# k loaded for two groups at a time in rows of two tokens, turned and pooled by head halves

## The chip, the cores and the metric

The kernel runs on one core of one Trainium2 chip. The metric is device time in microseconds, the median of several executions. Engines are named as the profile names them: PE multiplies matrices (PEld loads its weights), DVE, ACT and POOL work on tiles, and SP only issues DMAs.

## The reference, cut to what matters

Attention over keys and values that are averaged over eight tokens, then two feed-forward layers (the first one without an activation between its products):

```python
batch, n_heads, seq, head_dim = (8, 8, 576, 64)
k_p = k.reshape(B, H, Sp, pool, D).mean(axis=3)          # pool = 8, Sp = 72
v_p = v.reshape(B, H, Sp, pool, D).mean(axis=3)
scores = scale * np.matmul(q, k_p.transpose(0, 1, 3, 2))
scores = scores - np.max(scores, axis=-1, keepdims=True)
attn = np.exp(scores)
attn = attn / (np.sum(attn, axis=-1, keepdims=True) + 1e-09)
out = np.matmul(attn, v_p)                               # to 4608 tokens x 512
x = (x @ w1) * (x @ w2) @ w3 @ w_out                     # 512 -> 1024 -> 512
h = x @ w_in
x = (h * (1.0 / (1.0 + np.exp(-1.702 * h)))) @ w_out2    # 512 -> 2048 -> 512
```

All data are float32. q and k are drawn eight times wider than the other inputs.

## The kernel before, in words

**Groups.** Attention is worked in 32 groups; a group n is two heads of one batch element (`divmod(n, HP)` with four pairs of heads). The steps of a group are functions: `g_load` (k and q), `g0` (turn and pool k, turn q), `g1` (scores and their maximum), `g2` (exponential), `g3` (sum and division), `g_va` and `g_vb` (pooled values), `g4` (probabilities turned and split in two parts), `g6` (probabilities times values, written into the slots of x). `tick_first` and `tick` call them one after another, one tick at a time, between the steps of the weights.

**k in a group.** `load_blocks` (L229) issues four DMAs for k and four for q, each for 32 partitions: partition t holds token 32 g + t, for one head and one half of its 64 elements. So each piece of memory that is read is 32 floats, 128 bytes. DVE turns the 32 x 32 blocks (L255 for k, L256 for q), so that the head's elements lie on the partitions and the tokens along the row, and sums each eight tokens (L258). ACT copies the sums of head 0 and head 1 into a block matrix `kbd` (L260, L261), with zeros elsewhere, so that one product with the turned q gives the scores of both heads (L277).

```python
kbd = pa.tile([P, 2, SK], F32, name="kbd")
nc.scalar.copy(kbd[:D, 0], ks[:D])
nc.scalar.copy(kbd[D:, 1], ks[D:])
g_load(n + 1)
```

The raw k and q share one tag of four buffers, which is two groups of each. v is loaded by L249 and L250 into a single buffer, at the end of `g_va` of the group before.

**Weights.** At the same time `Conv` loads the weights (L151; 40 loads of 512 KB in this first stage, 24 with rows of 4 KB and 16 with pieces of 1 KB) and converts each on ACT (L166, L168), DVE (L169) and POOL (L172), then splits it in a high and a low part (L104 on ACT, L105 on DVE or POOL). Each product of two float32 matrices is three products of these parts (L114, L115, L116). The weight stage first multiplies w3 by w_out: w3 is turned on PE (L508), and for each of eight row blocks 24 products sum into one bank `acc`. Then the blocks of 512 tokens pass through w1, w2 and the product of the weights (the loop over `blk` and `f`, L602), with two ticks of attention in each step. The last stage, from about 600 us on, prepares and computes the second layer (`bk` in the rows).

**Order.** The instructions of each engine and the issues of each DMA queue are put in order when the kernel is built, by a scheduler that simulates the program's instructions with their dependences (`schedule_with_timeline_sim=True`). On the chip each engine runs its own list in that order and waits by semaphores. So a changed duration or dependence at one place can move instructions elsewhere. Nearly all DMAs are issued by SP.

Of the kernel before, what the change touches and what calls it, by code (L numbers as in the profile page):

```python
# [7 lines left out]
F32 = mybir.dt.float32  # L8
# [4 lines left out]
ALU = mybir.AluOpType  # L13
AX = mybir.AxisListType
# [3 lines left out]
P = 128  # L18
# [4 lines left out]
def pooled_attention_moe_moe2(  # L23
# [167 lines left out]
    with pa_ctx:  # L191
# [13 lines left out]
        nc.vector.memset(qT[:, S:], 0.0)  # L205
        kbd = pa.tile([P, 2, SK], F32, name="kbd")
        nc.vector.memset(kbd, 0.0)
        s_sl = take(dtype=F32)
# [15 lines left out]

        g_q, g_k, g_v, g_s = {}, {}, {}, {}

        def load_blocks(dst, src, b, hp):
            for c in range(4):
                nc.sync.dma_start(  # L229
                    dst[32 * c:32 * c + 32],  # L230
                    src[b, 2 * hp + c // 2, :, 32 * (c % 2):32 * (c % 2) + 32].rearrange(
                        "(g t) d -> t g d", t=32))

        def g_load(n):
            if n >= NG:
                return
            b, hp = divmod(n, HP)
            g_k[n] = pa.tile([P, S], F32, name="kr", tag="raw", bufs=4).rearrange("p (g d) -> p g d", d=32)
            load_blocks(g_k[n], k, b, hp)
            g_q[n] = pa.tile([P, S], F32, name="qr", tag="raw", bufs=4).rearrange("p (g d) -> p g d", d=32)  # L240
            load_blocks(g_q[n], q, b, hp)
# [10 lines left out]
        def g0(n):  # L252
            kr, qr = g_k.pop(n), g_q.pop(n)
            kT = pa.tile([P, S], F32, name="kT", tag="kT")
            nc.vector.transpose(out=kT, in_=kr.rearrange("p g d -> p (g d)"))  # L255
            nc.vector.transpose(out=qT[:, :S], in_=qr.rearrange("p g d -> p (g d)"))  # L256
            ks = pa.tile([P, SK], F32, name="ks", tag="ks")
            nc.vector.tensor_reduce(  # L258
                out=ks, in_=kT.rearrange("p (s u) -> p s u", u=POOL), op=ALU.add, axis=AX.X)
            nc.scalar.copy(kbd[:D, 0], ks[:D])  # L260
            nc.scalar.copy(kbd[D:, 1], ks[D:])  # L261
            g_load(n + 1)
# [7 lines left out]
        def g1(n):  # L270
            sc, s_t = banks_of(n), s_of(n)
            mov = kbd.rearrange("p a s -> p (a s)")
            nm = pa.tile([P, 2 * TT], F32, name="nm", tag="nm", bufs=2)
# [288 lines left out]

        conv.load()
        g_load(0)
        v_load(0)
# [563 lines left out]
```

## Time and profile before

| what | value |
|---|---|
| median of three runs | 1477.42 us (1476.0 to 1481.82) |
| the profiled execution | 1479.71 us, of which the span of the profile 1478.0 us |
| PE busy | 1438.7 us (97% of the span) |
| DVE, ACT, POOL busy | 988.7, 693.9 and 489.0 us |
| mean granted clock of PE | 0.993 of full speed |
| packets of the DMA engines | 294,436, of them 201,664 under 512 bytes |
| read and written in HBM | 209.72 and 56.62 MB |

The page of the profile gives the busy time of each engine, its busy tenths in 40 equal slices of the span, and the chain of work that ended last. "Releaser" is what ended an idle time. The DMA share is the mean busy share of the core's 16 DMA engines; it can be over 1 in a short stretch, since packets overlap.

### The profile page before, as it was taken

To read this page: it belongs to the slowest core of one execution; us is meant where nothing else is said; L and a number is where in the kernel's file an instruction comes from. 1 tells how busy PE (TensorE), PEld (TensorE's weight loads), DVE (VectorE), ACT (ScalarE), POOL (GpSimd) and SP (SyncE) were. 2 spreads that over 40 slices of the span, in tenths; PEclk is the share of its full clock that TensorE was granted. 3 is DMA by queue.
4 is the path that set the end of the run, shared out by engine and by line. 5 is a ranking of instruction groups with operands and counts; after the bars stand their busy time and mean duration, and the time that the engine had idled before them with its cause. 6 is when DMAs were issued, how large, how long until landed. Compare 5 with 4: busy or idle time off the path is not lost.

```text
span 1478.0 us, 19436 instructions
## 1 busy us (share of the span) xinstructions
PE 1438.7 (97%) x6536; PEld 1190.0 (81%) x6536; DVE 988.7 (67%) x1728; ACT 693.9 (47%) x1212; POOL 489.0 (33%) x589
## 2 busy tenths in 40 slices
PE   6979999999999999999999999999999999999998
PEld 4867888888888888888788887888788888888886
DVE  7888998878787877654737255683559354944554
ACT  7875444434343433366635344552455244534442
POOL 8789656554545555366733100000000000000000
PEclk9989999999999999999999999999999999999999
DMA  9992233323232311199879978877677766785665
GB/s 265 248 233 48 57 85 57 80 46 78 49 77 49 77 33 37 42 325 344 309 236 398 325 243 276 294 211 221 194 244 224 221 197 221 239 234 180 194 213 139
DMA packets 294436, 267.64 MB, mean 181 GB/s; under 512 B 201664, under 2 KB 226240, under 8 KB 294336
## 3 DMA queue, kind: packets, MB, share of 16 engines
q1 hardware_dynamic: 291648, 265.09, 59.8%
q10 hardware_dynamic: 2688, 1.31, 0.3%
q8 instruction: 52, 0.85, 0.2%
q14 instruction: 48, 0.39, 0.1%
HBM read 209.72 MB, written 56.62 MB: 180 GB/s over the span
## 4 chain that ended last, share of the span: by engine, by line
PE 82%; DMA 7%; DVE 5%; ACT 2%; SPq 2%; issue 1%; POOL 1%; DVEq 0%; ACTq 0%; POOLq 0%
PE bk L709 39%; PE wk L114 8%; PE wk L115 8%; PE wk L116 8%; PE acc L114 4%; PE acc L115 4%; PE acc L116 4%; PE wk L277 2%; DMA wud<-wt 2%; DVE p L314 1%; SPq L229 1%; DMA st<-wind 1%; PE bk L115 1%; PE bk L116 1%; PE bk L114 1%
## 5 line engine op out<-in xcount | busy, mean ns | idle before, releaser
L709 PE MATMUL bk<-mv,st 128*128 128x512 f32 x1152 | 272.6, 391 | 0.7 <-DMA st<-wud 0.7
L709 PE MATMUL bk<-xM,st 128*128 128x512 f32 x1092 | 259.0, 390 | 3.9 <-DMA st<-wind 3.7
L709 PEld LDWEIGHTS bk<-mv,st 128*128 128x128 f32 x1152 | 217.3, 189 | 46.3 <-issue 1.1
L709 PEld LDWEIGHTS bk<-xM,st 128*128 128x128 f32 x1092 | 204.5, 188 | 48.6 <-issue 2.5
L114 PE MATMUL wk<-s,s 128*128 128x512 f32 x576 | 227.0, 396 | 2.8 <-DVE a L641 1.2
L116 PE MATMUL wk<-s,s 128*128 128x512 f32 x576 | 224.9, 391 | 2.1 <-DVE s L105 2.1
L115 PE MATMUL wk<-s,s 128*128 128x512 f32 x576 | 224.9, 391 | 0.0
L314 DVE STREAM_TRANSPOSE p<-s_t 32x160 f32<-32x160 f32 (+1 forms) x560 | 178.5, 319 | 10.3
L114 PE MATMUL acc<-s,s 128*128 128x512 f32 x352 | 134.8, 406 | 8.2 <-ACT s L104 3.2
L115 PE MATMUL acc<-s,s 128*128 128x512 f32 x352 | 141.4, 402 | 0.9 <-POOL s L105 0.8
L116 PE MATMUL acc<-s,s 128*128 128x512 f32 x352 | 140.4, 399 | 0.0
L114 PEld LDWEIGHTS wk<-s,s 128*128 128x128 f32 x576 | 108.5, 189 | 26.2 <-DVE a L641 2.1
L116 PEld LDWEIGHTS wk<-s,s 128*128 128x128 f32 x576 | 108.3, 188 | 24.8 <-DVE s L105 2.3
L115 PEld LDWEIGHTS wk<-s,s 128*128 128x128 f32 x576 | 108.4, 188 | 22.1 <-DVE s L391 0.4
L105 DVE TENSOR_TENSOR mv<-g,mv 128x1024 fp32r<-128x1024 f32 x80 | 97.8, 1222 | 33.6 <-ACT mv L104 32.2
L104 ACT CAST mv<-g 128x1024 fp32r<-128x1024 f32 x80 | 84.3, 1054 | 71.8 <-PE bk L709 71.4
L172 POOL TENSOR_TENSOR cv<-cv,s 128x512 int32<-128x512 int32 x72 | 97.5, 1364 | 28.6 <-DVE cv L169 21.1
L105 POOL TENSOR_TENSOR s<-a,s 128x512 fp32r<-128x512 f32 x56 | 72.5, 1294 | 82.5 <-ACT s L104 62.7
L638 ACT COPY a<-wk 128x512 f32<-128x512 f32 x72 | 42.1, 585 | 110.5 <-PE wk L116 89.7
L369 POOL TENSOR_TENSOR ph<-p,ph 128x576 fp32r<-128x576 f32 x32 | 45.7, 1429 | 126.5 <-ACT ph L368 123.9
L114 PEld LDWEIGHTS acc<-s,s 128*128 128x128 f32 x352 | 67.8, 193 | 23.4 <-ACT s L104 5.2
L115 PEld LDWEIGHTS acc<-s,s 128*128 128x128 f32 x352 | 68.2, 194 | 15.0 <-POOL s L105 2.0
(190 smaller groups left out, 2357.9 us busy)
## 6 DMA issues: line engine op xcount, KB each, us to landing
st<-wud SPq DMA_DIRECT2D x96, 512.0 KB, 4.4
st<-wind SPq DMA_DIRECT2D x66, 512.0 KB, 4.7
st<-wind SPq DMA_DIRECT2D x76, 256.0 KB, 3.9
s<-in_moe_w_dram SPq DMA_DIRECT2D x32, 512.0 KB, 6.4
wind<-s SPq DMA_DIRECT2D x32, 512.0 KB, 5.4
s<-in_moe_w_out_dram SPq DMA_DIRECT2D x24, 512.0 KB, 6.5
kr<-in_k_dram SPq DMA_DIRECT2D x128, 72.0 KB, 2.6
qr<-in_q_dram SPq DMA_DIRECT2D x128, 72.0 KB, 2.6
```

The costliest lines, as they stand in the source:

```text
L104: nc.scalar.copy(dst[:, 0], src)
L105: lo_eng.tensor_tensor(out=dst[:, 1], in0=src, in1=f32(dst[:, 0]), op=ALU.subtract)
L114: nc.tensor.matmul(o, a[:, 0, a_sl], b[:, 0, b_sl], start=first, stop=False)
L115: nc.tensor.matmul(o, a[:, 0, a_sl], b[:, 1, b_sl], start=False, stop=False)
L116: nc.tensor.matmul(o, a[:, 1, a_sl], b[:, 0, b_sl], start=False, stop=last)
L172: nc.gpsimd.tensor_tensor(out=w.bitcast(I32), in0=w.bitcast(I32), in1=lo_w.bitcast(I32), op=ALU.add)
L229: nc.sync.dma_start(dst[32 * c:32 * c + 32], src[b, 2 * hp + c // 2, :, 32 * (c % 2):32 * (c % 2) + 32].rearrange("(g t) d -> t g d", t=32))
L277: nc.tensor.matmul(sc[half][:, i * KW:(i + 1) * KW], qT[:, sl(tt)], mov, start=True, stop=True)
L314: nc.vector.transpose(out=dst[:, :nt, 32 * c:32 * c + 32], in_=s_t[32 * c:32 * c + 32, :nt, 32 * r:32 * r + 32])
L369: nc.gpsimd.tensor_tensor(out=ph[:, 1], in0=s0, in1=f32(ph[:, 0]), op=ALU.subtract)
L638: nc.scalar.copy(a, pa_)
L709: nc.tensor.matmul(o, w[:, x, m], b[:, y], start=first and n == 0, stop=last and n == 2, skip_group_check=True)
```

## The change

k is loaded for two groups at a time, that is, for four heads. Each head has its own 32 partitions, and the partition t takes the tokens in pairs: one piece is two tokens of one head, 128 floats, 512 bytes (`k_load`). It is issued once for two groups, at the end of the k part of `g0` of the even group, into a single buffer; q keeps two buffers of its own and its old pieces. In `g0` of an even group both halves of the head (a = 0, 1) are turned and summed one after the other, for both groups. The sum now goes over two dimensions, since the tokens of a pool lie in two runs of four. Each group then copies four pieces of 32 x 72 into its block matrix, of which there are two, one for even and one for odd groups.

```diff
-        kbd = pa.tile([P, 2, SK], F32, name="kbd")
-        nc.vector.memset(kbd, 0.0)
+        kbds = [pa.tile([P, 2, SK], F32, name=f"kbd{i}") for i in range(2)]
+        for kbd in kbds:
+            nc.vector.memset(kbd, 0.0)
...
+        def k_load(i):
+            if i < NG // 2:
+                b, hq = divmod(i, HP // 2)
+                g_k[i] = pa.tile([P, S // 64, P], F32, name="kr", tag="kr")
+                for h in range(4):
+                    nc.sync.dma_start(
+                        g_k[i][32 * h:32 * h + 32],
+                        k[b, 4 * hq + h].rearrange("(g t e) d -> t g (e d)", t=32, e=2))
+
         def g_load(n):
...
-            g_k[n] = pa.tile([P, S], F32, name="kr", tag="raw", bufs=4).rearrange("p (g d) -> p g d", d=32)
-            load_blocks(g_k[n], k, b, hp)
-            g_q[n] = pa.tile([P, S], F32, name="qr", tag="raw", bufs=4).rearrange("p (g d) -> p g d", d=32)
+            g_q[n] = pa.tile([P, S], F32, name="qr", tag="raw", bufs=2).rearrange("p (g d) -> p g d", d=32)
...
         def g0(n):
-            kr, qr = g_k.pop(n), g_q.pop(n)
-            kT = pa.tile([P, S], F32, name="kT", tag="kT")
-            nc.vector.transpose(out=kT, in_=kr.rearrange("p g d -> p (g d)"))
+            if n % 2 == 0:
+                kr = g_k.pop(n // 2).rearrange("p g (e a d) -> p a (g e) d", e=2, a=2)
+                ks = g_ks[0] = pa.tile([P, 2, SK], F32, name="ks", tag="ks")
+                for a in range(2):
+                    kT = pa.tile([P, S], F32, name="kT", tag="kT")
+                    nc.vector.transpose(
+                        out=kT.rearrange("p (x t) -> p x t", t=32), in_=kr[:, a])
+                    nc.vector.tensor_reduce(
+                        out=ks[:, a].rearrange("p (g s) -> p g s", s=8),
+                        in_=kT.rearrange("p (g e s r) -> p g s e r", e=2, s=8, r=4),
+                        op=ALU.add, axis=AX.XY)
+                k_load(n // 2 + 1)
+            qr = g_q.pop(n)
             nc.vector.transpose(out=qT[:, :S], in_=qr.rearrange("p g d -> p (g d)"))
-            ks = pa.tile([P, SK], F32, name="ks", tag="ks")
-            nc.vector.tensor_reduce(
-                out=ks, in_=kT.rearrange("p (s u) -> p s u", u=POOL), op=ALU.add, axis=AX.X)
-            nc.scalar.copy(kbd[:D, 0], ks[:D])
-            nc.scalar.copy(kbd[D:, 1], ks[D:])
+            for c in range(4):
+                r = 32 * (2 * (n % 2) + c // 2)
+                nc.scalar.copy(
+                    kbds[n % 2][32 * c:32 * c + 32, c // 2], g_ks[0][r:r + 32, c % 2])
             g_load(n + 1)
...
-            mov = kbd.rearrange("p a s -> p (a s)")
+            mov = kbds[n % 2].rearrange("p a s -> p (a s)")
...
         conv.load()
+        k_load(0)
         g_load(0)
```

In the changed file the lines are numbered anew: the load of k is L240, that of q L230, those of v L257 and L258, the turn and the sum of k L266 and L268, the turn of q L274, the product for the scores L294 (before L277), the turn of the probabilities L368 to L378 (before L351 to L361), probabilities times values L397 to L400 (before L380 to L383).

**The order on SP** after the 18th weight load, in the weight stage. kr, qr, vr and vtr are the raw k, q and v; s_ and a number is a buffer that takes a weight; x4 means four DMAs in a row. Before:

```order
L229 DMA kr<-in_k_dram 32x18x32 x4
L229 DMA qr<-in_q_dram 32x18x32 x4
L249 DMA vr<-in_v_dram 128x512
L250 DMA vtr<-in_v_dram 16x512
L151 DMA s_412<-in_moe_w_dram 128x1024
L151 DMA s_447<-in_moe_w_dram 128x1024
```

With the change:

```order
L151 DMA s_562<-in_moe_w_dram 128x1024
L151 DMA s_657<-in_moe_w_dram 128x1024
L151 DMA s_688<-in_moe_w_dram 128x1024
L151 DMA s_766<-in_moe_w_dram 128x4x256
L230 DMA qr<-in_q_dram 32x18x32 x2
L240 DMA kr<-in_k_dram 32x9x128 x4
L230 DMA qr<-in_q_dram 32x18x32 x2
L257 DMA vr<-in_v_dram 128x512
L258 DMA vtr<-in_v_dram 16x512
```

These are the loads of q for group 2 and of v for group 1. They stood behind 18 weight loads and now stand behind 25; with them comes k of groups 2 and 3.

**The order on DVE** where group 0 is turned (kT, qT: turned k and q; ks: its sums; L169 and L105 belong to the weights). Before:

```order
L255 STREAM_TRANSPOSE kT<-kr 128x576
L169 TENSOR_SCALAR cv<-cv 128x512
L105 TENSOR_TENSOR s_339<-cv,s_339 128x512
L258 TENSOR_REDUCE ks<-kT 128x72
L256 STREAM_TRANSPOSE qT<-qr 128x576
```

With the change:

```order
L266 STREAM_TRANSPOSE kT<-kr 128x576
L169 TENSOR_SCALAR cv<-cv 128x512
L105 TENSOR_TENSOR s_339<-cv,s_339 128x512
L268 TENSOR_REDUCE ks<-kT 128x72
L274 STREAM_TRANSPOSE qT<-qr 128x576
L266 STREAM_TRANSPOSE kT<-kr 128x576
L268 TENSOR_REDUCE ks<-kT 128x72
```

The second half's turn and sum stand behind the turn of q; both sums are needed for group 0's block matrix.

**The order on PE** at the end of the weight stage (ident: a turn of the probabilities; ph, vm and pt, vt: probabilities times values; acc_66 with L114 to L116: the last block of 24 products of the weight stage, of which the first rows are shown). Before:

```order
L360 MATMUL acc_68<-ident,s_126 32x128
L361 MATMUL acc_68<-ident,s_126 32x64
L383 MATMUL wk_72<-pt,vt 128x288
L383 MATMUL wk_73<-pt,vt 128x288
L114 MATMUL acc_66<-s_192,s_1046 128x512
L115 MATMUL acc_66<-s_192,s_1046 128x512
L116 MATMUL acc_66<-s_192,s_1046 128x512
```

With the change:

```order
L377 MATMUL acc_68<-ident,s_128 32x128
L378 MATMUL acc_68<-ident,s_128 32x64
L400 MATMUL wk_72<-pt,vt 128x288
L400 MATMUL wk_73<-pt,vt 128x288
L397 MATMUL acc_69<-ph,vm 128x288
L397 MATMUL acc_68<-ph,vm 128x288
L114 MATMUL acc_66<-s_194,s_1042 128x512
L115 MATMUL acc_66<-s_194,s_1042 128x512
L116 MATMUL acc_66<-s_194,s_1042 128x512
```

The first products of probabilities and values of group 3 now stand ahead of that block; before, they stood behind its 24 products (there as L380).

## Rows read from the trace of the kernel before

**Rows 1.** The page, the span in 40 equal slices: busy tenths, DMA share.

```profile
PE   6979999999999999999999999999999999999998
...
DMA  9992233323232311199879978877677766785665
```

**Rows 2.** Windows: start:end, us, busy PE, PEld, DVE, ACT, POOL (instructions), clock, DMA share, GB/s.

```profile
0.00:126.50 126.50, 101.44 (x460) 78.65 (x460) 103.62 (x170) 97.80 (x199) 102.66 (x118) 0.93 0.89 223
126.50:700.00 573.50, 572.18 (x2724) 482.04 (x2725) 443.75 (x1040) 247.86 (x538) 322.08 (x424) 1.00 0.35 93
700.00:1478.00 778.00, 765.04 (x3354) 629.30 (x3352) 441.37 (x520) 348.28 (x475) 64.27 (x48) 1.00 0.74 239
```

**Rows 3.** Timeline of SP's queue: start us, us, issuing line, DMA, number merged.

```profile
51.82 8.80 SPq L229 DMA_DIRECT2D kr<-in_k_dram  x4
...
102.39 1.54 SPq L151 DMA_DIRECT2D s<-in_moe_w_dram  x3
...
303.41 2.06 SPq L229 DMA_DIRECT2D kr<-in_k_dram  x4
```

**Rows 4.** DMA, 0 to 110 us: packets, MB, share; issues with KB each, us to landing.

```profile
q1 hardware_dynamic: 52449, 27.39, 98.2%
...
kr<-in_k_dram SPq DMA_DIRECT2D x36, 72.0 KB, 6.0
qr<-in_q_dram SPq DMA_DIRECT2D x32, 72.0 KB, 3.5
```

**Rows 5.** Chain that ended last, 86 to 127 us: shares, then start us, us, what.

```profile
by line: SPq L229 16.0%; DVE p L314 14.7%; DMA vr<-in_v_dram 11.0%; DVE s L105 8.4%; DVE cv L169 8.4%; DMA qr<-in_q_dram 7.5%; issue 6.5%; DVE a L641 2.9%; POOL va L324 2.6%; DVE s_t L284 2.3%; DVE wk L300 2.0%; DVE s_t L303 2.0%; DVE s L39
...
88.30 4.52 DMA vr<-in_v_dram
92.89 1.07 POOL va L324
```

**Rows 6.** Windows with k and q, and with weights in 1024-byte pieces, columns as in rows 2.

```profile
303.50:309.50 6.00, 6.00 (x32) 5.13 (x31) 2.83 (x6) 2.32 (x5) 1.14 (x2) 1.00 0.62 100
618.50:624.50 6.00, 6.00 (x29) 5.03 (x28) 0.67 (x1) 2.54 (x4) 3.60 (x3) 1.00 0.53 175
```

**Rows 7.** Groups of instructions, 0 to 126 us: busy us, mean ns, idle before.

```profile
L255 DVE STREAM_TRANSPOSE kT<-kr 128x576 f32<-128x576 f32 x8 | 6.1, 768 | 1.6 <-DMA kr<-in_k_dram 1.6
...
L258 DVE TENSOR_REDUCE ks<-kT 128x72 f32<-128x576 f32 x7 | 5.2, 739 | 0.0
...
L260 ACT COPY kbd<-ks 64x72 f32<-64x72 f32 x7 | 1.8, 254 | 3.7 <-DVE ks L258 3.5
...
L340 ACT CAST vt<-vtf 32x64 fp32r<-32x64 f32 x4 | 0.9, 233 | 0.0
```

**Rows 8.** Timelines of ACT and PE in the calm stretch, copies and their use.

```profile
285.77 0.25 ACT L261 COPY kbd<-ks 64x72 f32<-64x72 f32 x1
...
300.80 1.39 PE L277 MATMUL wk<-kbd,qT 128*128 128x144 f32 x10
```

**Rows 9.** Window of 10 us, columns as in rows 2.

```profile
110.00:120.00 10.00, 9.72 (x44) 7.95 (x43) 9.92 (x22) 7.52 (x15) 9.63 (x10) 0.90 0.36 67
```

**Rows 10.** Timeline of PE: start us, us, what, and idle time ahead with its releaser.

```profile
70.41 1.39 PE L277 MATMUL acc<-kbd,qT 128*128 128x144 f32 x10
...
74.26 0.40 PE L116 MATMUL acc<-s,s 128*128 128x512 f32 x1
...
94.02 0.50 PE L114 MATMUL acc<-s,s 128*128 128x512 f32 x1 [1.36 <-DVE s L105]
...
101.53 0.40 PE L115 MATMUL acc<-s,s 128*128 128x512 f32 x1
101.76 0.40 PE L116 MATMUL acc<-s,s 128*128 128x512 f32 x1
...
103.08 0.39 PE L380 MATMUL acc<-ph,vm 128*128 128x288 f32 x1
...
107.79 0.50 PE L116 MATMUL wk<-s,s 128*128 128x512 f32 x1 [2.06 <-DVE s L105]
```

More of the change, by code (lines that the diff above doesn't have):

```diff
@@ L222, in pooled_attention_moe_moe2 @@
         nc.gpsimd.memset(f32(vt), 0.0)
-        g_q, g_k, g_v, g_s = {}, {}, {}, {}
+        g_q, g_k, g_ks, g_v, g_s = {}, {}, {}, {}, {}
         def load_blocks(dst, src, b, hp):
```

## Prediction

> **What bounds the kernel now.** I read the 40 slices of the page first [rows 1]. TensorE (PE) is at nine tenths or more in all but the first three and the last, and the DMA engines are full in the first three and again from the eighteenth on. So the first 110 us are a stage of their own. The windows cut the span in three [rows 2]: up to 126.5 us PE is busy for 101.4 us, which leaves 25.1 us idle; from 126.5 to 700 us it idles 573.5 - 572.2 = 1.3 us; after 700 us it idles 13.0 us. The 32 groups lie in the first two stretches, so the change works there, and only the first has time to give. The granted clock there is 0.93 on average, and full in the other two.
>
> What the first stretch waits for is in the queue of SyncE (SP) [rows 3]: the four loads of one group's k take 8.80 us to issue there, against 2.06 us in the calm stretch. They wait for room. The DMA view of the first 110 us [rows 4] says why: one queue keeps the 16 engines busy for 98.2%. The chain from 86 us on goes through the same place [rows 5]: its largest share is the issue of k and q (L229), and the load of v that stands behind k is waited for by POOL. Of the last of the 40 weight loads, the issue ends at 103.9 us [rows 3].
>
> **Price of a transfer.** Four loads of k and four of q, 590 KB in pieces of 128 bytes, take 0.62 x 6 = 3.72 us of all 16 engines [rows 6]. That is 1.86 us for k of a group, 0.465 us for one load. In the same view 1.05 MB in pieces of 1024 bytes take 0.53 x 6 = 3.18 us. No row has 512 bytes. By piece, that is 3.72/288 = 12.9 ns and 3.18/64 = 49.7 ns on one engine; on the straight line between, 512 bytes cost 28.7 ns. A pair of groups has 1152 such pieces, 72 for each engine: 2.06 us, in place of 3.72 us. The ends: 1.79 us at the rate of the 1024-byte row, 3.72 us if the bytes cost what they do now. I take 2.06 us, since it lies between measured sizes on both sides.
>
> A rule speaks for a smaller gain. The Trainium skill, "DMA: Bandwidth & Descriptors", section "Why small descriptors are slow (HBM only)", charges a piece one cycle per 32 bytes and about three more, so 19 cycles for 512 bytes against 7 for 128. By it a pair would cost 72 x 19 / (288 x 7) = 0.68 of 3.72, an estimate of 2.5 us, and the sum below would come out 2 to 3 us smaller. The trace's two rows speak against its proportions: 1024 bytes cost 49.7/12.9 = 3.9 times 128 bytes, where it says 5.
>
> **The DMA term.** By the order on SP, the 40th weight load stands behind 32 loads each of k and q (eight groups) and five of v now; afterwards behind 20 loads of k (five pairs), 28 of q and six of v. So k goes from 8 x 1.86 = 14.9 us to 5 x 2.06 = 10.3 us, q falls by 4 x 0.465 = 1.9 us, and a v, 0.295 MB in long pieces, adds 0.9 us at the 1024-byte rate: 5.6 us less. In the crowded stage a load costs more: 108 us of queue time, less 22.4 MB of the rest at the 1024-byte rate (67.7 us), leaves 40.3 us for 68 loads, 0.59 us each [rows 4], 1.27 times the calm price. With that factor it is 7.1 us. I take the middle, 6.4 us. The ends: 2.7 us more (a pair at 3.72 us), 8.9 us less (1.79 us, and the factor).
>
> **How much of it arrives.** While the queue is full, nothing else is idle for long: up to 126.5 us DVE is busy 103.6, POOL 102.7 and ACT 97.8 us [rows 2], and from 110 to 120 us DVE is busy for 9.92 of 10 us [rows 9]. Weights that come earlier must still be converted there; DVE's 22.9 us of idle time hold 6 us, but not every microsecond finds its gap. I count four fifths: 5.1 us.
>
> **ACT and DVE.** The copies into the block matrix go from two of 64 x 72 (0.254 us) to four of 32 x 72; the nearest row, 32 x 64, has 0.233 us [rows 7]. That is 4 x 0.24 - 0.51 = 0.45 us more on ACT for a group, 3.2 us for the seven groups up to 126.5 us. ACT has 28.7 us idle there; I count an eighth, 0.4 us (ends: 0 and 3.2). The transposes and sums of k stay as many: two of 0.77 and two of 0.74 us a pair [rows 7], on the same 576 elements. Their strided reading has no row; the bound is zero to a tenth of 0.77 us, hidden. But group 0 now waits for both halves, so its scores stand behind one transpose and one sum more, 1.5 us, which group 1 gets back. Half of it, 0.8 us, I put on the path. The second block matrix is cleared before any data arrive: nothing.
>
> **What is hidden.** From 126.5 to 600 us each group costs ACT 0.45 us more, and SP issues four loads of k for a pair in place of eight. PE waits for neither: in the calm stretch the copies into the block matrix end at 286.0 us and PE uses them at 300.8 us [rows 8], so 14.8 us cover them and the 1.5 us of DVE work that now comes in pairs. If that cover were gone, 0.45 us a group over 25 groups would be 11 us. The single buffer of a pair is loaded again right behind its transposes and needed two groups later; its wait stands ahead of q and v on SP, but is for a transpose just done.
>
> After 700 us the scheduler's order on SP and PE differs in places too, though nothing there was edited. PE idles 13.0 us there [rows 2]; I count no change, with a quarter of it, 3 us, either way.
>
> **The sum:** -5.1 + 0.4 + 0.8 = -3.9 us. The profiled execution took 1479.71 us (span 1478.0 and 1.7 around it), 2.3 us above the median of the three runs, 1477.42. Against that median I expect 1473.5 us.
>
> **Rivals.**
> (1) The stage gives more. The full 8.9 us arrive, and with shorter stalls some of the half-clock time (the 0.93) comes back, 1 to 3 us: 1466 us. For it: the load of v of group 3, for which POOL waits [rows 5], stands behind 12 loads of k and 36 weights in place of 28 and 34: 28 x 0.465 - 12 x 0.515 - 2 x 1.59 = 3.7 us sooner. Against: DVE is full from 110 to 120 us.
> (2) The transfers were hidden anyway, or stay 128 bytes in fact: DVE and POOL set the end of the stage, the earlier weights wait in their buffers, and ACT's 3.2 us eat the rest. -1 to +2 us: 1478 us. For it: the three engines' busy times. Against: L229 leads the chain.
> (3) Slower, through PE's order. The scheduler has put group 2's q and v behind seven more weight loads, and the first products of weights and values for group 3 (L380, afterwards L397) ahead of the last block of 24 products of the weight stage, which stood before them. PE runs in order: if group 3's probabilities or values are late, those 24 and all that follow wait. Before, group 3 needed from its scores at 70.4 us to 103.1 us for that product, while PE used the time from 94.0 us for the block [rows 10]. If the chain keeps its 33 us and the scores start at 74.3 us, where PE has done the 144 products of the weight stage that now stand ahead of them [rows 10], the product comes at 107 us and the 24 behind it (24 x 0.23 = 5.5 us by the starts in rows 10) end at 112.5 us, where they ended by 102.0: 10.5 us, less the 2.1 us that PE waits at 107.8 us anyway, +8.4 us, 1486 us. It decides from the moment that this product comes later than about 98 us (102.0 + 2.1 - 5.5). Against: v of group 3 is issued sooner.
>
> **How the numbers follow.** Forecast 1473.5 us, chance 0.42; rival (1) 0.25, (2) 0.20, (3) 0.13. A measurement of this kernel can tell about 0.5%, 7.4 us, from no change: 1470.0 and 1484.8 us are the marks. Below the first lie rival (1) and the lower edge of the forecast, 0.30; above the second most of rival (3), 0.12; between, 0.58. The forecast's own range is 1469 to 1478 us. The whole range, 1465 to 1484 us, takes in rivals (1) and (2), the DMA term's ends and the 3 us of the tail, and leaves out some 0.06 below and 0.12 above.
>
> **What would show it.** Right: the packets under 512 bytes fall by 73,728, the loads of k on SP go from 128 to 64 and the issue of the last weight load ends near 98 us in place of 103.9; PE's idle time up to about 125 us falls by 4 us from 25.1; from there to 700 us it stays under 2 us; the copies on ACT number 128 and last 0.24 us each. The step on what arrives is wrong if the last weight comes 6 us sooner and PE's idle time does not follow. The price is wrong if a calm pair of k takes over 3 us of the engines. Rival (3) shows as an idle stretch of over 5 us on PE ahead of L397 between 90 and 110 us. The forecast as a whole falls if PE idles over 3 us between 130 and 600 us.

## The result, and the profile after

The changed kernel takes 1490.43 us (median of 6 runs, 1488.93 to 1495.15), the kernel before, timed beside it, 1479.12 us: ratio 1.0081, 95% interval 1.0065 to 1.0097. It is slower by 0.8%, and the prediction (1473.5 us, at most 1484) was wrong. A median below is that of a kernel's own runs; ratios are against runs of the kernel before on the same chip, and leave disturbed runs out, so they can differ a little from those of the medians.

The slices of the page after, as in [rows 1], with the granted clock:

```profile
PE   5978999999999999999999999999999999999998
...
PEclk9979999999999999999999999999999999999999
DMA  9962222323232311079969979868667766785665
```

DMA has lost the load that it was meant to lose (third slice 6, not 9; packets under 512 bytes 126,912 in place of 201,664). PE is not busier for it. The windows after, columns as in [rows 2]:

```profile
0.00:126.50 126.50, 97.87 (x433) 74.01 (x434) 97.44 (x160) 102.03 (x218) 103.35 (x123) 0.91 0.79 225
126.50:700.00 573.50, 565.85 (x2677) 474.69 (x2677) 439.42 (x1039) 248.12 (x566) 310.61 (x411) 0.99 0.30 83
```

Up to 126.5 us PE is idle for 28.6 us in place of 25.1, and from there to 700 us for 7.65 us in place of 1.3. It also does less while it is busy: the same two windows for 90 to 110 us, first of the kernel after, then of the kernel before.

```profile
90.00:100.00 10.00, 6.08 (x23) 3.57 (x21) 6.94 (x13) 9.29 (x24) 8.88 (x11) 0.58 0.54 146
100.00:110.00 10.00, 7.49 (x20) 5.75 (x21) 4.88 (x8) 5.73 (x13) 9.69 (x13) 0.57 0.10 32
```

```profile
90.00:100.00 10.00, 8.64 (x35) 6.53 (x34) 6.46 (x10) 8.32 (x18) 7.94 (x10) 0.83 0.98 231
100.00:110.00 10.00, 7.54 (x37) 5.84 (x36) 9.83 (x12) 6.86 (x16) 9.40 (x12) 0.93 1.19 249
```

The DMA share fell from 1.19 to 0.10 while PE did 20 matmuls in place of 37, at a clock of 0.57: most of that time at 1.2 GHz, the lower of its two levels, after it had stood idle in pieces. A useful measure for such a stage is work done by a given time. Matmul instructions of the lines 114 to 116 (the products of the weight stage and of the x stage, which is the blocks of 512 tokens behind it; about 0.23 us each at full clock), each counted in one window from 0 to the time given:

| by (us) | before | after |
|---|---|---|
| 80 | 144 | 157 |
| 100 | 193 | 174 |
| 120 | 242 | 212 |
| 150 | 357 | 316 |
| 220 | 614 | 550 |
| 300 | 921 | 853 |
| 500 | 1689 | 1625 |

At 80 us the change is ahead by 13 products. By 150 us it is 41 behind, by 220 us 64, and from there on the gap stays at 60 to 70. Nearly all of the loss is made between 80 and 220 us. The first matmul behind the x stage, which I use as a mark, shows the same:

```profile
L116 PE MATMUL bk<-mv,wo x64: 389/389/389, 774.4 to 852.0; 128*128 128x512 f32 x64
```

```profile
L116 PE MATMUL bk<-mv,wo x64: 389/389/389, 791.6 to 868.7; 128*128 128x512 f32 x64
```

From 774.4 us before to 791.6 us after: 17.2 us late. What follows the mark takes 703.6 us before and 698.9 after, so 4.7 us come back in the tail and 12.5 us of span remain. In the kernel after, the queue that was full now waits. Its timeline on SP, columns as in [rows 3]:

```profile
92.11 0.39 SPq L151 DMA_DIRECT2D s<-in_moe_w_dram  x1
96.09 1.81 SPq L240 DMA_DIRECT2D kr<-in_k_dram  x4
...
108.84 1.77 SPq L151 DMA_DIRECT2D s<-in_moe_w_dram  x2
```

This load of k takes 1.8 us to issue (8.80 us in [rows 3]), but the last two weights leave at 108.8 us. SP's waits from 90 to 111 us (us in total, times, longest) say what stands ahead of them: k waits for its single buffer, v for its own, and the last weights 4.7 us for products of the weight stage, which free their slots.

```profile
SPq L151 <- PE acc L116: 5.6, 2, 4.7
SPq L240 <- DVE kT L266: 3.4, 1, 3.4
SPq L257 <- POOL va L341: 3.3, 1, 3.3
```

VectorE (DVE) now stands on its own k. Its timeline, and its waits over the whole run:

```profile
95.30 0.77 DVE L266 STREAM_TRANSPOSE kT<-kr 128x576 f32<-128x576 f32 x1
96.10 0.75 DVE L268 TENSOR_REDUCE ks<-kT 128x72 f32<-128x576 f32 x1
96.77 0.86 DVE L169 TENSOR_SCALAR cv<-cv 128x512 uint32<-128x512 uint32 x1
101.93 0.78 DVE L266 STREAM_TRANSPOSE kT<-kr 128x576 f32<-128x576 f32 x1 [4.30 <-DMA kr<-in_k_dram]
102.63 0.65 DVE L105 TENSOR_TENSOR s<-acc,s 128x512 fp32r<-128x512 f32 x1
```

```profile
DVE kT L266 <- DMA kr<-in_k_dram: 35.7, 12, 4.3
```

The second turn of a pair frees the only k buffer at 96 us, SP reloads it (96.09), and three rows further on DVE's own order wants the refill: it waits 4.30 us, and the eviction of weight products that stands behind (L105) waits with it. PE then waits for that eviction, ahead of the last block of the weight stage, and runs the first half of it at half speed (starts 0.43 us apart up to 108.6 us, then 0.23). PE's timeline:

```profile
99.98 0.85 PE L397 MATMUL acc<-ph,vm 128*128 128x288 f32 x2 [0.18 <-ACT p L376]
103.34 0.79 PE L114 MATMUL acc<-s,s 128*128 128x512 f32 x1 [2.51 <-DVE s L105]
103.93 0.63 PE L115 MATMUL acc<-s,s 128*128 128x512 f32 x1
104.36 0.63 PE L116 MATMUL acc<-s,s 128*128 128x512 f32 x1
```

That block began at 94.02 us before [rows 10].

### The profile page after: what moved, and what is told of

It reads as the page before. It is cut to its first block, busy times and chain, and to the rows that moved or that the text cites. A ratio compares the mean times of both kernels' runs of the same rounds, so it can differ in the third digit from the quotient of the medians.

```text
span 1490.5 us, 19393 instructions
## 1 busy us (share of the span) xinstructions
PE 1443.7 (97%) x6536; PEld 1190.9 (80%) x6536; DVE 983.5 (66%) x1729; ACT 708.4 (48%) x1276; POOL 487.8 (33%) x589
## 2 busy tenths in 40 slices
DMA packets 238115, 267.63 MB, mean 180 GB/s; under 512 B 126912, under 2 KB 169920, under 8 KB 238016
## 4 chain that ended last, share of the span: by engine, by line
PE 79%; DVE 9%; DMA 7%; ACT 2%; issue 1%; SPq 1%; POOL 0%; DVEq 0%; ACTq 0%; POOLq 0%
PE bk L727 38%; PE wk L114 7%; PE wk L115 7%; PE wk L116 7%; PE acc L114 4%; PE acc L115 4%; PE acc L116 4%; DVE p L331 3%; DMA wud<-wt 2%; PE wk L294 2%; DMA kr<-in_k_dram 2%; PE bk L114 1%; PE bk L115 1%; PE bk L116 1%; DMA qr<-in_q_dram 1%
## 5 line engine op out<-in xcount | busy, mean ns | idle before, releaser
L114 PE MATMUL wk<-s,s 128*128 128x512 f32 x576 | 228.5, 398 | 8.1 <-DVE a L659 5.9
L116 PE MATMUL wk<-s,s 128*128 128x512 f32 x576 | 226.0, 394 | 0.2 <-DVE s L105 0.2
L114 PE MATMUL acc<-s,s 128*128 128x512 f32 x352 | 133.0, 402 | 9.1 <-ACT s L104 5.5
L116 PE MATMUL acc<-s,s 128*128 128x512 f32 x352 | 140.4, 399 | 0.0
L114 PEld LDWEIGHTS wk<-s,s 128*128 128x128 f32 x576 | 108.8, 189 | 33.7 <-DVE a L659 8.5
L116 PEld LDWEIGHTS wk<-s,s 128*128 128x128 f32 x576 | 109.0, 189 | 23.4 <-DVE s L105 0.6
L105 DVE TENSOR_TENSOR mv<-g,mv 128x1024 fp32r<-128x1024 f32 x80 | 97.7, 1222 | 33.4 <-ACT mv L104 32.0
L105 POOL TENSOR_TENSOR s<-a,s 128x512 fp32r<-128x512 f32 x56 | 72.5, 1294 | 85.2 <-ACT s L104 83.4
L114 PEld LDWEIGHTS acc<-s,s 128*128 128x128 f32 x352 | 67.6, 193 | 25.1 <-ACT s L104 8.3
L385 ACT CAST ph<-p 128x576 fp32r<-128x576 f32 x32 | 21.5, 673 | 125.9 <-DVE p L331 125.9
L116 PEld LDWEIGHTS acc<-s,s 128*128 128x128 f32 x352 | 67.7, 192 | 15.1 <-DVE s L105 1.4
```

The costliest lines, as they stand in the source:

```text
L105: lo_eng.tensor_tensor(out=dst[:, 1], in0=src, in1=f32(dst[:, 0]), op=ALU.subtract)
L114: nc.tensor.matmul(o, a[:, 0, a_sl], b[:, 0, b_sl], start=first, stop=False)
L116: nc.tensor.matmul(o, a[:, 1, a_sl], b[:, 0, b_sl], start=False, stop=last)
L385: nc.scalar.copy(ph[:, 0], s0)
```

## The experiments

All of them in one table, with before and after: median, ratio with its interval, the mark, and PE's idle time in two windows. The mark and the idle times are those of the one profiled run of each kernel, which lies up to 5.2 us from the median (changed_v_first 4.5 us below it, anchor_early 5.2 and own_pair1_anchor 3.8 us above).

| kernel | us | ratio | mark | idle to 126 | 126 to 300 |
|---|---|---|---|---|---|
| before | 1479.12 | 1 | 774.4 | 24.6 | 1.8 |
| after | 1490.43 | 1.0081 (1.0065 to 1.0097) | 791.6 | 28.6 | 7.7 |
| anchor_all | 1488.54 | 1.0068 (1.0046 to 1.0090) | 784.0 | 27.5 | 3.4 |
| anchor_late | 1489.50 | 1.0072 (1.0051 to 1.0093) | 787.3 | 29.4 | 5.9 |
| anchor_early | 1488.94 | 1.0074 (1.0050 to 1.0098) | 790.4 | 27.8 | 7.2 |
| four_copies | 1495.62 | 1.0121 (1.0095 to 1.0147) | 793.9 | 36.3 | 7.7 |
| copies_late | 1477.47 | 0.9991 (0.9977 to 1.0004) | 772.9 | 26.7 | 0.8 |
| copies_g2 | 1477.72 | 1.0000 (0.9987 to 1.0013) | 775.8 | 27.3 | 2.6 |
| copies_g3 | 1494.53 | 1.0123 (1.0099 to 1.0148) | 791.9 | 38.1 | 4.8 |
| two_blocks | 1485.38 | 1.0042 (1.0027 to 1.0058) | 781.3 | 29.5 | 4.2 |
| v_first | 1474.35 | 0.9970 (0.9956 to 0.9984) | 773.8 | 28.2 | 0.1 |
| q_first | 1485.81 | 1.0048 (1.0032 to 1.0063) | 780.5 | 29.6 | 2.4 |
| one_k_buffer | 1490.59 | 1.0089 (1.0072 to 1.0106) | 785.8 | 31.0 | 2.5 |
| changed_v_first | 1489.84 | 1.0075 (1.0058 to 1.0092) | 785.9 | 25.6 | 8.1 |
| anchor_v_first | 1482.97 | 1.0028 (1.0017 to 1.0039) | 782.0 | 28.4 | 4.3 |
| one_block | 1496.74 | 1.0127 (1.0114 to 1.0140) | 794.7 | 30.2 | 9.9 |
| k_256 | 1476.59 | 0.9990 (0.9976 to 1.0004) | 771.5 | 26.0 | 1.2 |
| kq_256 | 1472.40 | 0.9964 (0.9948 to 0.9980) | 770.4 | 22.5 | 1.2 |
| own_pair1 | 1489.76 | 1.0078 (1.0064 to 1.0092) | 786.7 | 32.7 | 4.2 |
| own_pair1_anchor | 1480.61 | 1.0027 (1.0014 to 1.0039) | 780.5 | 30.0 | 0.6 |

The theories by their numbers: (1) DVE stalls on the single k buffer; (2) the loss is the weight stage alone, whose last block comes late and at half clock; (3) the four small copies cost it; (4) the order of the rows costs it, whatever has moved them; (5) the second block matrix does; (6) the single buffer does, through the bunched groups.

**Is it the stall on the single k buffer?** A 1x1 copy (the anchor) that writes a corner of the last kT behind every odd group's q turn keeps the next pair's turn behind it, some 30 us after its load.

```
             nc.vector.transpose(out=qT[:, :S], in_=qr.rearrange("p g d -> p (g d)"))
+            if n % 2:
+                nc.vector.tensor_copy(g_ks[1][:1, :1], qT[:1, :1])
```

Here `g_ks[1]` is the last kT of the pair. anchor_late has `n % 2 and n > 4`, anchor_early `n % 2 and n < 4`.

> The changed kernel, with one 1x1 copy on VectorE behind every odd group's q turn that writes a corner of the last kT, so that the next pair's k turn can stand only behind it, some 30 us behind its load instead of 4. Theory 1 (VectorE stalls in its own order on the single kr buffer: 12 waits, 35.7 us in the changed kernel): the waits for kr fall under 5 us, TensorE's idle time between 126.5 and 700 us falls from 7.65 to under 2.5 us, and the time from 1490.4 to 1479 to 1484 us. Theory 2 (the loss is the weight stage alone: its last 24 products stand behind group 3's probabilities-times-v and run at half clock): the waits go, but the time stays at 1487 to 1491 us. Theory 3 (the four small ScalarE copies a group cost it): stays at 1489 to 1491 us.

> The same copy, but only from group 5 on: the order up to the third pair's k turns, which is most of the weight stage, stays that of the changed kernel, and the stalls from 100 us on go. Theory 1: as with the copy everywhere, within 2 us, 1479 to 1484 us, since 11 of the 12 stalls lie behind 100 us. Theory 2: 1487 to 1491 us. If the two anchored kernels differ by over 3 us, the weight stage's order has a price of its own.

> The same copy, but only behind groups 1 and 3: the order of the weight stage changes as with the copy everywhere, and the stalls behind it stay. Theory 1: the waits for kr stay at 30 to 36 us and the time at 1486 to 1491 us. Theory 2: if the copy mends the weight stage's order, the time falls to 1480 to 1484 us although the stalls stay.

The waits go, and the time hardly follows: 1.0068, with an interval that overlaps that of the change. What is left of them in anchor_all, in DVE's waits:

```profile
DVE s L105 <- DMA kr<-in_k_dram: 0.4, 1, 0.4
```

So 35 us of waits on an engine were not 35 us of the kernel's time: the medians differ by 2 us, and the two intervals leave room for some 6 at most. Theory 1 fell in the form in which I had put it (6 to 11 us back). anchor_early does the same with the stalls still in (38.3 us of them), so the three kernels don't tell a price of the stalls from none. Theory 2's range (1487 to 1491 us) holds all three, but the table of products speaks against the weight stage alone: the changed kernel is 30 products behind by 120 us and 64 by 220.

**Is it the four small copies?** The kernel before with nothing but the split:

```
-            nc.scalar.copy(kbd[:D, 0], ks[:D])
-            nc.scalar.copy(kbd[D:, 1], ks[D:])
+            for c in range(4):
+                nc.scalar.copy(kbd[32 * c:32 * c + 32, c // 2], ks[32 * c:32 * c + 32])
```

> The kernel before, with its two copies of 64 rows a group split into four of 32 rows and nothing else changed. By the changed kernel's rows four copies take 0.25 us each, against 0.51 us for two before, so ScalarE has about 0.5 us a group, 15 us in all, more. Theory 3 (the copies are on the path): 1483 to 1492 us. Theories 1 and 2 (ScalarE has room, at 5 of 10 us busy behind the weight stage): 1477 to 1481 us, no change.

1495.6 us, slower than the whole change and above theory 3's own range: theory 3 seemed right. But the program's scheduler orders the rows of each engine by its own estimates, and by the traces hundreds of rows of TensorE's order differed. So the same split came again where it moves no row of the weight stage: behind `if n < 6` the old copies, from group 6 on the four (26 of 32 groups). Some 50 rows of TensorE still change places, the first of them at 154 us.

> The kernel before, with the four small copies in place of two only from group 6 on. The rows of the weight stage stand as in the kernel before on every engine; 26 of 32 groups still pay the copies. Theory 3 (the copies' time is on the path): 26/32 of the loss with four copies everywhere (18.9 us), 1490 to 1494 us. Theory 4 (the loss is the new order in which the weight stage's rows stand on the engines, whatever has moved them): 1476 to 1479 us, no change.

0.9991: 26 groups' copies cost nothing that can be told. Then the split in one group only, once in group 2 and once in group 3 (`if n != 2` and `if n != 3` keep the old copies). The added work is the same; only in group 3 do the rows move.

> The kernel before, with four small copies in place of two in group 2 alone, inside the weight stage. ScalarE does 0.45 us more there, and no other row changes its place. Theory 4: 1476 to 1479 us, no change. If ScalarE is on the path in this stage, at most 0.5 us more, which is under what can be told.

> The kernel before, with four small copies in place of two in group 3 alone: the same 0.45 us as in group 2, but here the rows behind it come to stand in another order (some 380 rows of TensorE's order and 180 of VectorE's differ). Theory 4: 3 us or more away from the kernel before, to either side, 1470 to 1498 us, for the same work. If work and not order decides: 1476 to 1479 us, as with group 2.

1.0000 and 1.0123. Two small copies more cost nothing in one place and 17 us in the other. This is the pair on which the verdict rests, so here is where it shows: DVE's timeline, first with the split in group 2, then in group 3. L395 evicts group 3's result, L318 is the block of 20 turns of group 4's probabilities.

```profile
111.15 0.45 DVE L395 TENSOR_TENSOR s<-acc,s 128x288 fp32r<-128x288 f32 x1
...
112.21 0.35 DVE L395 TENSOR_TENSOR s<-acc,s 128x224 fp32r<-128x224 f32 x1
...
118.79 6.65 DVE L318 STREAM_TRANSPOSE p<-s_t 32x160 f32<-32x160 f32 x20
```

```profile
118.06 6.65 DVE L318 STREAM_TRANSPOSE p<-s_t 32x160 f32<-32x160 f32 x20
...
127.23 0.74 DVE L395 TENSOR_TENSOR s<-acc,s 128x288 fp32r<-128x288 f32 x2
```

The evictions have changed sides with a block of 6.65 us. PE waits for them, at the lower clock. From the timeline and a window of PE with the split in group 3, and the same window with the split in group 2:

```profile
128.03 0.80 PE L115 MATMUL wk<-s,s 128*128 128x512 f32 x1 [5.72 <-DVE s L395]
```

```profile
120.00:130.00 10.00, 3.78 (x9) 1.91 (x8) 9.76 (x22) 4.34 (x9) 7.30 (x9) 0.50 0.18 30
```

```profile
120.00:130.00 10.00, 8.89 (x43) 7.12 (x41) 9.73 (x25) 5.94 (x14) 8.23 (x9) 1.00 0.02 3
```

PE does 9 matmuls in these 10 us in place of 43. This is the longest wait, not the only one: from 100 to 120 us PE idles 8.6 us with the split in group 3 and 2.3 us with it in group 2, in pieces of up to 2.7 us. How the scheduler came to swap the two I did not look into.

**How wide is the spread of orders?** Three more edits of the kernel before that add no work, or next to none: two block matrices by turns, group 0's v issued ahead of its k and q, and q ahead of k in every group. The fourth does the v edit in the changed kernel.

```
+        kbds = [pa.tile([P, 2, SK], F32, name=f"kbd{i}") for i in range(2)]
...
-        g_load(0)
-        v_load(0)
+        v_load(0)
+        g_load(0)
...
-            load_blocks(g_k[n], k, b, hp)
...
             load_blocks(g_q[n], q, b, hp)
+            load_blocks(g_k[n], k, b, hp)
```

> The kernel before with two block matrices taken by turns in place of one, and nothing else: no instruction is added but one more memset, and one wait (the next group's copies for the scores of this one) is gone. Rows change places on TensorE only behind about its 250th. Theory 3: 1475 to 1479 us, no change. Theory 4: the early rows keep their places, so at most 3 us to either side, 1474 to 1480 us. A loss of over 4 us would say that the second block matrix itself, and not the loads or copies, costs the time.

> The kernel before, with group 0's v issued ahead of its k and q: the same instructions with the same durations, only the rows of the weight stage come to stand in another order. Theory 3 and any other by which work that was added costs the time: 1475 to 1480 us. Theory 4: the time leaves this range, by the size that the other reorderings showed, 1483 to 1497 us; a fall below 1473 us would say that the order is worth as much the other way.

> The kernel before with each group's q issued ahead of its k: the same instructions with the same durations in another order. Theory 4: outside 1474.5 to 1479.5 us, to either side, by 3 to 20 us. If work that was added were the cause and order nothing, 1475 to 1479 us. With v first, the other reordering without work, it was 1474.4 us, with two block matrices 1485.4 us; a third value says how wide the spread is.

> The changed kernel, with group 0's v issued ahead of k and q: the same instructions in another order. Theory 3: 1487 to 1492 us, as the changed kernel. Theory 4: another time than the changed kernel's by over 3 us to either side, anywhere from 1473 to 1500 us; how much faster it can get says whether the change's gain in loads is there to be had.

1.0042, 0.9970 and 1.0048. Reordering without work moves this kernel by -0.3% to +0.5%, a spread as wide as the loss. Three of the expectations missed: v_first gained, where I had expected a loss; two_blocks lost 8.5 us, where theory 4 gave it 3 at most, and by its own sign this pointed to the second block matrix (theory 5, tried next); and in the changed kernel the v edit changes nothing that can be told, 1.0075, where theory 4 wanted over 3 us. Its profiled run, the fastest of its six, is ahead on the weight stage (232 products by 120 us in place of 212) and still behind the kernel before: 339 by 150 us against 357, 664 by 240 us against 687.

**Is it the single buffer or the second block matrix?** One block matrix in the changed kernel (`kbds[0]` for `kbds[n % 2]`); one k buffer in the kernel before:

```
-            g_k[n] = pa.tile([P, S], F32, name="kr", tag="raw", bufs=4).rearrange("p (g d) -> p g d", d=32)
+            g_k[n] = pa.tile([P, S], F32, name="kr", tag="kr", bufs=1).rearrange("p (g d) -> p g d", d=32)
-            g_q[n] = pa.tile([P, S], F32, name="qr", tag="raw", bufs=4).rearrange("p (g d) -> p g d", d=32)
+            g_q[n] = pa.tile([P, S], F32, name="qr", tag="raw", bufs=2).rearrange("p (g d) -> p g d", d=32)
```

> The changed kernel with one block matrix in place of two: loads, turns, sums and copies stay, and the next group's copies again wait for this group's scores. Theory 4 (the loss is the order in which the rows of the first 300 us stand): the rows change places again, 1474 to 1498 us, no side excluded. Theory 5 (the second block matrix is the cause, since in the kernel before it alone cost 8 us and lets the next group's copies and scores in ahead of the weight stage's products): 1478 to 1484 us, that is 6 to 12 us back.

> The kernel before with one k buffer in place of k's share of four: no instruction is added or grows, but k's loads are held until the turn ahead of them has been done, and VectorE's order brings the next k turn 3 to 5 rows behind. Theory 1 in its weaker form (a single buffer that is refilled just ahead of its use stalls VectorE): waits for kr of 30 to 90 us in all on VectorE, and a loss of 3 to 12 us. Theory 4: the rows move, 1474 to 1498 us, and the loss shows as products that are late at 150 us, not in the waits for kr.

Theory 5 fell: with one block matrix it is 1496.7 us, slower still. One k buffer alone costs the kernel before 1.0089, as much as the whole change, with 4.9 us of waits for kr in place of the 30 to 90 expected: the loss came without the stall, as products that are late (302 by 150 us against 357). What the two kernels share stands in their order: in the kernel before, 201 products of the weight and x stages stand ahead of group 3's probabilities times v, and groups 1 to 3 stand behind 144, 164 and 201. With one k buffer it is 171, 171 and 174, in the changed kernel 157, 174 and 174, ahead of the stage's last 24 products. That was theory 6, tried from both sides. (The 240 and 220 products in the first text below are sums over windows, in which a product that runs across an edge counts twice; counted once they are 232 and 212.)

> The changed kernel with both the 1x1 copy behind every odd group's q turn (no waits for kr on VectorE) and v ahead of group 0's k and q. With v first alone the last weights were issued at 98.6 us and 240 products were done at 120 us against 220, and the stalls on kr then cost it what it had gained between 150 and 300 us. If the stalls cost that: the first matmul behind the x stage, at 785.9 us with v first alone, comes at 776 to 781 us, and the time is 1477 to 1483 us. If the stalls are cover here too, 1487 to 1491 us. Under theory 4 alone nothing can be said ahead: 1474 to 1498 us.

> The changed kernel, in which the second pair (groups 2 and 3) has a buffer of its own, two slots that the weights don't need yet, and is loaded where the kernel before loads group 2's k. Theory 6 (the single pair buffer holds the second pair's load until the first pair has been turned; groups 1 to 3 then finish in a bunch, group 3's probabilities-times-v ahead of the last 24 products of the weight stage, as one k buffer alone did to the kernel before): in the order, group 3's product is behind all of the stage's products again, so the last eviction of the stage comes at 103 to 108 us in place of 117, the first matmul behind the x stage at 778 to 785 us in place of 791.6, and the time is 1478 to 1485 us, with the stalls on kr behind 100 us still in it. Without theory 6: 1487 to 1498 us.

> The same with the 1x1 copy behind every odd group's q turn, so that no turn of k waits for its load. Theory 6: the last eviction of the stage at 103 to 108 us, TensorE's idle time between 126 and 300 us under 3 us, the first matmul behind the x stage at 773 to 780 us, and 1473 to 1479 us in all, level with the kernel before or up to 4 us under it. Without theory 6: 1485 to 1492 us, as with the copy alone.

The edit of own_pair1 (this pair's load is then eight DMAs, and its turns read two pieces):

```
+                if i in OWN:                      # OWN = (1,)
+                    g_k[i] = [take(dtype=F32) for _ in range(2)]
...
+            if n % 2 and n // 2 + 1 in OWN:
+                k_load(n // 2 + 1)
```

anchor_v_first takes 1483.0 us, at the upper end of its range, with the mark at 782.0 us, just behind it. own_pair1 missed: group 3's product is behind 201 products again, and the kernel still takes 1489.8 us. Its idle time to 126 us even rises to 32.7 us. With the anchor added it is 1480.6 us, 1.0027, also above its range. The anchor alone, the buffer alone and v first alone each bring back nothing that can be told from none; anchor and v first, or anchor and buffer, bring back two thirds of the loss (1.0081 to 1.0028 and 1.0027). Group 3's row alone is therefore not the cause, and no version of the change that I ran is as fast as the kernel before.

**What are lighter loads worth, with the order held?** k in rows of 256 bytes, then k and q. No row moves on any engine or queue. The scores are those of other values of k (and q), since a load brings 288 tokens with all 64 columns.

```
-            load_blocks(g_k[n], k, b, hp)
+            for c in range(4):
+                nc.sync.dma_start(
+                    g_k[n][32 * c:32 * c + 32].rearrange("p (x g) d -> p x (g d)", x=9),
+                    k[b, 2 * hp + c // 2, S // 2 * (c % 2):S // 2 * (c % 2 + 1)].rearrange(
+                        "(g t) d -> t g d", t=32))
```

> The kernel before, with k's loads in rows of 256 bytes in place of 128: as many loads of as many bytes, half the packets, each row one token's whole head. The k that reaches the turn is another one (every 32 partitions hold all 64 columns of 288 tokens, not 32 columns of all 576), so this kernel computes scores of other values in the same time. No row of any engine or queue changes its place against the kernel before. This is the load term of the prediction alone, with the order held. If the queue bounds the first 104 us, as the prediction had it, and four fifths of the saving arrive: k's price falls by 1.86 us less what 256-byte rows cost, some 0.6 to 0.9 us a group over about 8 groups, so 4 to 6 us less: 1471 to 1474 us. If the queue has room that nobody waits for, 1476 to 1479 us.

> The same for k and q: both in rows of 256 bytes, with other values, and no row in another place. It removes twice as many packets as the step above, about as many under 512 bytes as the change and half as many again. If the queue bounds the first 104 us: 8 to 12 us less, 1465 to 1470 us, and the last weights issued by 98 us. If not: within 2 us of the step above.

k alone: 0.9990, -1.5 us of 1477.5 with an interval from -3.5 to +0.6. k and q: 0.9964, -5.3 us (-7.7 to -3.0). The queue over the first 110 us, k alone and then both (52449 packets at 98.2% before, [rows 4]):

```profile
q1 hardware_dynamic: 43381, 27.83, 99.2%
```

```profile
q1 hardware_dynamic: 34561, 27.99, 95.4%
```

With k alone the queue is as full as before; the room was taken by other loads. A calm window of that kernel, with k and q of one group:

```profile
318.50:325.00 6.50, 6.50 (x32) 5.45 (x31) 3.70 (x7) 2.45 (x7) 1.69 (x2) 1.00 0.48 91
```

They take 0.48 x 6.5 = 3.12 us, and q alone 1.83 (below), so k costs about 1.3 us a group in place of 1.86: 8 x 0.56 = 4.5 us less load in the stage, of which some 1.5 us, or nothing, arrive. The same window with both lightened:

```profile
318.00:324.50 6.50, 6.50 (x33) 5.57 (x32) 3.32 (x7) 2.50 (x5) 1.65 (x2) 1.00 0.39 91
```

Here k and q take 0.39 x 6.5 = 2.5 us in place of 3.7, some 9 us less load over eight groups, and 5.3 us of it (3.0 to 7.7) arrive. This fits neither expectation: 1472.4 us lies above 1465 to 1470, and 4.2 us under k_256, where a queue that nobody waits for would have left it within 2. So the queue does bound the stage in part: lightened by 4.5 us it brings nothing that can be told, lightened by twice as much over half of it.

## Why the prediction was wrong, point by point

**The bound** was read rightly as to place (the first 126 us), too simply as to cause. The queue was full, but DVE, POOL and ACT were busy for about four fifths of the time too, and PE needs all of them in one order. With the order held, lighter loads brought 1.5 us (k) and 5.3 us (k and q): the end waits for the queue in part. That a queue is full does not show how much.

**The price of a pair** was right. A calm window of the kernel after with k and q, and one with q alone:

```profile
320.00:328.50 8.50, 8.50 (x42) 7.21 (x41) 5.15 (x9) 3.93 (x13) 4.01 (x6) 1.00 0.48 106
340.00:346.00 6.00, 6.00 (x31) 5.12 (x31) 2.80 (x7) 4.11 (x13) 2.89 (x4) 1.00 0.31 49
```

The queue in the same two windows (packets, MB, share of the 16 engines):

```profile
q1 hardware_dynamic: 3584, 0.89, 47.3%
q1 hardware_dynamic: 2368, 0.30, 30.5%
```

That is 4.02 us and 1.83 us, so 2.19 us for a pair, where I had 2.06 us. A piece of 512 bytes takes 2.19/72 = 30.4 ns, 2.4 times one of 128 bytes. The Trainium skill, "DMA: Bandwidth & Descriptors", section "Why small descriptors are slow (HBM only)", charges a piece one cycle per 32 bytes and about three more, from which an estimate for the two sizes is 19 to 7 cycles, 2.7 times. The trace agrees better here than at 1024 bytes; the rule is a little too dear again.

**How much of it arrives** ("I count four fifths") failed in the changed kernel, where nothing arrived: PE's idle time to 126.5 us rose by 3.5 us where it should have fallen by 4, and the last weight's issue ends at 110.6 us, not 98. It waited for a slot by then, not for the queue. With the order held the fraction was too high rather than wholly wrong: 1.5 of 4.5 us at k_256, not told from nothing, and 5.3 of some 9 us at kq_256, where four fifths lie within the interval. This step alone would have made the change worth less, not slower.

**ACT and DVE** were right in what the work takes: 128 copies of 0.249 us, which cost nothing that can be told where no row of the weight stage moves (copies_late, copies_g2); the turns on strided input take 0.77 us, as before. The 0.4 and 0.8 us of the sum are less than a run can tell.

**What is hidden** failed too, by the sentence on the single buffer: it "is loaded again right behind its transposes and needed two groups later", and its wait on SP "is for a transpose just done". The scheduler put the next turn three rows behind the load, where DVE waits 4.30 us, and SP waits 3.4 us for the transpose, with v and the last weights behind it. The rows of DVE's order show this, and I had not looked for it there. PE then idles 7.65 us between 126.5 and 700 us, over the 3 us at which I had said the forecast falls.

**Rival (3)**, with 0.13, is what came nearest. Group 3's product came at 99.98 us, behind its point of decision of 98 us; the last block of the weight stage stood behind it and began at 103.3 us in place of 94.0; the price was 8.4 us forecast, 12.5 us of span measured. The one idle stretch of over 5 us that was to show it did not come; there were several of 1 to 2.5 us, and a lower clock. And own_pair1 shows that this row alone is not the cause.

**The step that failed** is the sum itself: "-5.1 + 0.4 + 0.8" adds the change's work to the old order of the rows. The new order, which the rows of SP, DVE and PE ahead of the prediction showed and rival (3) took up, stands in it at nothing. An order has a price of its own: with the same work the kernel before takes 17 us more by it (copies_g3 against copies_g2), and reorderings without work move it by -0.3% to +0.5%. The changed kernel's 17.2 us at the mark are 9.7 us more idle time (4.0 of it up to 126 us, 5.8 from there to 300) and 7.5 us more busy time for as many matmuls, at the lower clock: ahead of the mark the trace has TensorE at its lower level for 30.7 us in place of 17.1, most of the difference in one stretch:

```profile
91.60:108.70 17.10, 11.46 (x33) 8.06 (x34) 9.49 (x17) 13.42 (x32) 16.47 (x21) 0.50 0.28 84
```

Shown: in the kernel before, the time follows the order of the rows in the first 220 us, with the same work. Shown: with the order held, the copies cost nothing that can be told, and lighter loads give 0 to 8 us, so neither can cost 12. Not shown: that the order alone makes up the changed kernel's 12 us. Its own loads, strided turns and sums were never run in the old order, so this is inferred. Open: which of its rows cost them. The stall on the single k buffer may be a part, since with the anchor the better orders gain 0.5% each (changed_v_first against anchor_v_first, own_pair1 against own_pair1_anchor); but the anchor moves hundreds of rows as well, and with the change alone it gained 0.1%, so stall and order are not told apart.

## What to carry to other kernels

Where a scheduler orders the rows, an edit has two effects, its work and a new order, and the second can be many times the first (17 us for two more copies of 0.25 us here): build a version in which no row moves, and measure the work in that. Where a buffer is single, look in the engine's order how many rows lie between the instruction that frees it and the one that reads the refill. A saturated queue is a bound only as far as lightening it, with everything else in place, brings the end forward: here a third, or none, of what k alone gave up, and over half of what k and q did.

If this kernel is to be sped up, v first in the kernel before is the one version that beats both and computes the same values: 1474.35 us, 0.9970 (0.9956 to 0.9984).

## What the runs showed that I had not expected

A copy of 32 x 72 takes as long on ACT as one of 64 x 72, 0.249 us each: splitting this copy by rows doubles its cost. Twelve waits of an engine, 35.7 us in all, could be taken out for 0.1% that can't be told from none. And idle time on TensorE came with a lower clock: in the changed kernel it is granted 0.58 and 0.57 between 90 and 110 us, and 0.50 between 120 and 130 us in copies_g3, each time after and between waits for other engines, DVE most of all, so that the products left to do took nearly twice their time as well.
